# Second products of five groups by seven half-size products instead of eight blocks, with a new order of units around them

## The chip, the cores and the metric

The kernel runs on one core of a Trainium2 chip. The metric is the device time of one execution in microseconds; before the change it is 712.18 us (median of three runs, 710.34 to 712.77). The engines are written as the profile has them: PE multiplies matrices (PEld loads its weights), DVE and ACT do elementwise work and empty the PSUM banks, POOL and SP issue DMAs.

## The reference, cut to what matters

```python
mod = (silu(c) @ w_mod).reshape(c.shape[0], 6, 1, -1)
sa, ca, ga, sb, cb, gb = (mod[:, n] for n in range(6))
h = layernorm(x) * (1 + ca) + sa
x = x + ga * A(h)            # y = Re(DFT_seq(DFT_hidden(h))), as four matrix products
h = layernorm(x) * (1 + cb) + sb
x = x + gb * B(h)
# B: gate = h @ w1; up = h @ w3; out = (silu(gate) * up) @ w2
```

S = 2048 rows, D = 512, F = 1792, all float32. The change lies in B alone: in the product with w2, which this text calls the second product. The products with w1 and w3 are the first products.

## The kernel before

Every operand of a product is split into a high part (a rounding to the PE's format, written by ACT) and a low part (the rest, by a subtraction on DVE), and each product is three passes: high x high, high x low, low x high (line 100). In B the 1792 columns are seven groups g of 256, the rows four tiles t of 512, taken as two pairs: pair 0 is tiles 0 and 2, pair 1 is tiles 1 and 3. Twelve of the fourteen (g, pair) are **items**, which run last: item 0 to 4 are groups 2 to 6 of pair 0, item 5 to 11 are groups 0 to 6 of pair 1. Item 5 is called `turning` in the code.

The first products of an item use Strassen's scheme in Winograd's form: `factor` (line 1239 on) makes seven products for w1 (named a1 to a7 here, `kind` "a") and seven for w3 (b1 to b7), each of six 128x512 matmuls. Products 1, 6, 7, 4 add up in one PSUM bank (a **chain**), 5 and 3 in another, 2 in a third. Between two members of a chain the partial sum is taken out of the bank: after 1, 5 and 6 by an ACT copy to a tile `x`, after 2, 3 and 7 by a DVE addition, after 4 by the consumer itself. So the next member waits for the engine that empties the bank. `weight_jobs` prepares the weights of that scheme: `h` and `l` (the raw weight), and `sh` and `sl` (four sums of quarters, made by `totals` on DVE).

The second product of an item is eight blocks (`down_unit`): for each of two tiles and four output blocks d, two inner halves of three passes, six matmuls into one bank. ACT scales the bank by gb into half of a tile y (line 335); after every second block POOL issues a DMA that adds y (512 KB) to the running sum of the output in DRAM (`sums`, line 1146). Groups 5 and 6 of pair 1 (`own`) don't go through DRAM: DVE adds them to tiles `xr`, which SP reads back from `sums` once group 4 is through (`load_sums`), and which SP stores to the output at the end.

What is called a **unit** here is six 128x512 matmuls: a first product or a block y. The order of units is written out by hand, item by item, in the strings `head` and `body` near the end ("a6 a5 y a7 y y ...": a and b are first products, "-b7" is one of the item before, y the next second product in the queue `seconds`). Each unit issues its matmuls, then what empties its bank; `behind(n, f)` puts a piece of work n units later; `jobs` is a queue of weight preparation from which `beside` takes as DVE and ACT have credit. Tiles are slots of 4 KB per partition, 50 in all, given back and taken again in turn; whoever writes into a slot waits for the last reader of the tile before, which for a y is its DMA. `down_banks` names the banks of the second product (6 and 7 in this part).

Of the kernel before, what the change touches and what calls it, by code (L numbers as in the profile page):

```python
# [8 lines left out]
F32 = mybir.dt.float32  # L9
# [33 lines left out]
def folded(nc, pools, c, cp, wmr, wmc, x, xt, ctr, cti, wdr, wdi, w1, w3, w2, out):  # L43
# [51 lines left out]
    def times(dst, a, b):  # L95
        nc.vector.tensor_tensor(out=dst, in0=a, in1=b, op=OP.mult)  # L96
# [1013 lines left out]
        nc.sync.dma_start(to, sums[t, i])  # L1110

    ys = {}
    down_banks = [4, 4]

    def down_unit(g, pair, t, d, key):
        last = g == NG - 1

        own = pair == 1 and g >= NG - 2
        if not own and d % 2 == 0:
            ys[0] = take(F32, "y")  # L1120

        parts = 2 if own and last and (t, d) == (NT - 1, ND - 1) else 1
        for n in range(parts):
            at = slice(n * N // parts, (n + 1) * N // parts)
            to = bank(down_banks[0] + turn[1] % down_banks[1])[:, at]
            turn[1] += 1
            for q in range(2):
                product(
                    to,
                    [u[:, q, cols(d)] for u in wuse[key]],  # L1130
                    [hf[g, t, q][:, b, at] for b in range(2)],
                    q == 0,
                    q == 1,
                )
            if own:
                xs = xr[t][d // 2][:, d % 2, at]
                nc.vector.scalar_tensor_tensor(
                    xs, to, gb[:, d : d + 1], xs, op0=OP.mult, op1=OP.add
                )
# [68 lines left out]
    TO = {1: 0, 6: 0, 7: 0, 4: 0, 2: 1, 5: 2, 3: 2}  # L1208
    state, vs = {}, {}

    def right(pair, n):
        t0, t1 = PAIRS[pair]
        if n in (1, 2, 3):
            at = {1: (t0, 0), 2: (t0, 1), 3: (t1, 1)}[n]
            return h2h[at], h2l[at]
        at = pair, {5: 1, 6: 2, 7: 3, 4: 4}[n]
        return th[at], tl[at]

    def result(i, w, q, k, src):

        g, pair = items[i]
        v = vs[i][q][:, k, :]
        if w == "w1":
            behind(k != 0 or q == 0, lambda: nc.scalar.activation(v, src, AF.Silu))  # L1224
            return
        times(v, v, src)

        def highs():
# [8 lines left out]
        behind(2, lows)  # L1237

    def factor(i, w, n):
# [37 lines left out]
        if n == 3:  # L1277
            for x in wuse.pop(key).values():
                give(x)
            behind(1, lambda: give(st["x"]))  # L1280
            if w == "w3":
                for x in vs.pop(i):
                    behind(3, lambda x=x: give(x))


    loads.extend((n, m) for n in range(len(steps)) for m in range(2))
# [289 lines left out]
                up_block(g, t, q, w)  # L1576
                beside(2.72, USED[w])

    def down(g, pair, t, d, key):
        drain(lambda: (key, "l") in done, jobs)  # L1580
        delayed()
        down_unit(g, pair, t, d, key)
        beside(1.36, USED["own" if pair == 1 and g >= NG - 2 else "y"])

    for w in ("w1", "w3"):
# [17 lines left out]
        give(h.pop((2, 0)))  # L1603


    down_banks[:] = [6, 2]
# [4 lines left out]
    def other_operands():  # L1611
# [6 lines left out]
                give(h.pop((0, n)))  # L1618
        sum_parts(jobs, *sums_of.pop())

    def unit(kind, i, n):
        g, pair = items[i]
        more = i + 1 < len(items)
        if n == 1:
            drain(lambda: ("ready", i, "w1" if kind == "a" else "w3") in done, jobs)
        if (kind, i, n) == ("a", 0, 6):
            drain(lambda: ("t", 0, 4) in done)
        if (kind, i, n) == ("a", turning, 1):
            drain(lambda: not background)
        if kind == "a" and i == turning and n in (4, 5, 6, 7):  # L1630
            drain(lambda: ("t", 1, {6: 2, 5: 1, 7: 3, 4: 4}[n]) in done, jobs)
        delayed()
        factor(i, "w1" if kind == "a" else "w3", n)
        if (kind, n) == ("a", 1) and more:
            load_w(("w1", *items[i + 1]))
        if (kind, n) == ("a", 6):
            load_w(("w2", g, pair))
        if (kind, n) == ("a", 3) and more:
            load_w(("w3", *items[i + 1]))
            weight_jobs(i + 1, "w1")  # L1640
        if (kind, n) == ("b", 2):
            plain_jobs(("w2", g, pair))
        if (kind, n) == ("b", 3):
            if i + 2 == turning:
                drain(lambda: ("xc", 3) in done)
                for at in ((1, 0), (1, 1), (3, 1)):
                    chunk_parts(background, *at, 3)
                sums_of.append(pair_sums(background, 1))
            if i + 1 == turning:
                other_operands()  # L1650
            if more:
                weight_jobs(i + 1, "w3")
            for t in PAIRS[pair]:
                seconds.extend((g, pair, t, d, ("w2", g, pair)) for d in range(ND))
        beside(1.36, FACTOR[kind][n])

    weight_jobs(0, "w3")
# [822 lines left out]
```

## Time and profile before

| | us |
|---|---|
| three runs | 710.34, 712.77, 712.18 |
| median | 712.18 |
| profiled execution | 708.46 |
| its span, first to last instruction | 706.7 |
| mean granted PE clock over the span | 0.991 |
| PE busy in the span | 686.3 |
| DVE busy | 548.3 |
| ACT busy | 430.8 |

The profile comes from one execution with its own time, so changes are worked out against its span and then set against the median. A group line of the profile has the line and engine, output <- input by tile names, the partitions x elements, the count, then busy time and the mean of one in ns. A timeline line has the start, the duration and the instruction. The last instruction that computes starts at 698.8 us; what follows is the store of the output.

### The profile page before, as it was taken

The page shows a single profiled execution, that of the slowest core. Times are in us where ns is not written, and L with a number is a line of the kernel's source. Part 1 is how long each engine was busy: PE and PEld are TensorE (multiplying, and loading weights), DVE is VectorE, ACT ScalarE, POOL GpSimd, SP SyncE. Part 2 cuts the span into 40 slices and gives each one's busy share as a digit, 9 for nine tenths or more (in the row PEclk, how much of TensorE's full clock was granted, in tenths as well). Part 3 has the DMA queues.
Part 4 walks back from the last instruction along what each step waited for, and adds up shares of the span by engine and source line. Part 5 has one row for each costly group of instructions (what it writes and reads, how often), then busy time and mean ns, then how long its engine had stood idle before and what let it go on. Part 6 is the DMA issues. An engine that isn't in the chain of part 4 may idle for free.

```text
span 706.7 us, 8912 instructions
## 1 busy us (share of the span) xinstructions
PE 686.3 (97%) x3152; PEld 564.7 (80%) x3152; DVE 548.3 (78%) x877; ACT 430.8 (61%) x709; POOL 119.4 (17%) x141
## 2 busy tenths in 40 slices
PE   7999999999999999899999999999999999999995
PEld 4898888888888888687888788787788888888784
DVE  5999679997999978579987886896865556664763
ACT  4998865545454655745677676867665565656420
POOL 1320253542524000200100101011010100101000
PEclk9999999999999999999999999999999999999998
DMA  8730299796678521522868558376763847537403
GB/s 266 211 120 1 77 373 328 251 307 229 207 283 287 168 86 41 92 58 64 209 114 199 89 130 153 61 156 137 239 136 73 180 62 175 111 69 162 137 0 124
DMA packets 38100, 108.93 MB, mean 154 GB/s; under 512 B 4896, under 2 KB 5152, under 8 KB 38048
## 3 DMA queue, kind: packets, MB, share of 16 engines
q0 software_dynamic: 12352, 43.00, 29.3%
q1 hardware_dynamic: 25264, 63.98, 27.5%
q10 hardware_dynamic: 432, 1.31, 0.5%
q8 instruction: 26, 0.43, 0.3%
q14 instruction: 26, 0.21, 0.1%
HBM read 76.81 MB, written 33.55 MB: 156 GB/s over the span
## 4 chain that ended last, share of the span: by engine, by line
PE 81%; DVE 7%; ACT 6%; issue 2%; DMA 2%; SPq 1%; ACTq 0%; DVEq 0%
PE bank L100 52%; PE bank L750 25%; PE bank L559 2%; PE bank L598 1%; DMA wmr<-in_wmr 1%; ACT xc L894 1%; PE bank L576 1%; DVE xc L96 1%; SPq L231 1%; ACT hf L87 1%; ACT y L335 1%; DVE v L96 0%; DVE hl L90 0%; ACT hm L501 0%; DMA w<-in_wdi 0%
## 5 line engine op out<-in xcount | busy, mean ns | idle before, releaser
L100 PE MATMUL bank<-hf,w2h 128*128 128x512 f32 (+1 forms) x452 | 140.9, 391 | 0.3
L1146 POOL DMA_DIRECT2D sum<-y x48 | 41.0, 855 | 390.1 <-ACT y L335 373.0
L100 PEld LDWEIGHTS bank<-hf,w2h 128*128 128x128 f32 x452 | 84.3, 188 | 22.1 <-DVE hf L90 3.4
L100 PE MATMUL bank<-hf,w2l 128*128 128x512 f32 (+1 forms) x226 | 87.6, 388 | 0.0
L87 ACT ACTIVATE hf<-v 128x512 fp32r<-128x512 f32 x56 | 35.3, 630 | 67.3 <-DVE v L96 62.7
L335 ACT ACTIVATE y<-bank,gb 128x512 f32<-128x512 f32 x96 | 64.9, 682 | 18.6 <-PE bank L100 18.3
L93 DVE TENSOR_TENSOR v<-bank,x 128x512 f32<-128x512 f32 x36 | 24.7, 685 | 34.9 <-PE bank L100 34.8
L750 PE MATMUL bank<-bh,us 128*128 128x512 f32 x128 | 49.9, 390 | 0.0
L93 DVE TENSOR_TENSOR x<-bank,x 128x512 f32<-128x512 f32 x36 | 24.7, 687 | 32.4 <-PE bank L100 28.7
L750 PE MATMUL bank<-bh,ul 128*128 128x512 f32 x128 | 49.8, 389 | 0.0
L750 PE MATMUL bank<-d,us 128*128 128x512 f32 x128 | 49.8, 389 | 0.0
L750 PE MATMUL bank<-d,uh 128*128 128x512 f32 x128 | 49.8, 389 | 0.0
L750 PE MATMUL bank<-l,us 128*128 128x512 f32 x128 | 49.8, 389 | 0.0
L750 PE MATMUL bank<-l,uh 128*128 128x512 f32 x128 | 49.8, 389 | 0.0
L100 PEld LDWEIGHTS bank<-hf,w2l 128*128 128x128 f32 x226 | 42.4, 188 | 8.4
L90 DVE TENSOR_TENSOR hf<-v,hf 128x512 fp32r<-128x512 f32 x56 | 38.5, 687 | 12.2 <-ACT hf L87 12.1
L170 POOL DMA_INDIRECT re<-in_ctr,mirror x32 | 35.8, 1117 | 66.2 <-DVE ul L90 39.5
L1224 ACT ACTIVATE v<-v 128x512 f32<-128x512 f32 x36 | 22.8, 632 | 38.8 <-DVE v L93 38.8
L87 ACT ACTIVATE x<-bank 128x512 f32<-128x512 f32 x72 | 41.4, 586 | 7.2 <-PE bank L100 6.5
L170 POOL DMA_INDIRECT im<-in_cti,mirror x32 | 32.7, 1023 | 35.3 <-PE bank L750 10.0
L100 PE MATMUL bank<-h2h,w1h 128*128 128x512 f32 x80 | 31.8, 397 | 1.5 <-ACT h2h L87 1.5
L100 PE MATMUL bank<-h2l,w1h 128*128 128x512 f32 x80 | 31.9, 399 | 0.8 <-DVE h2l L90 0.8
(246 smaller groups left out, 1775.2 us busy)
## 6 DMA issues: line engine op xcount, KB each, us to landing
sum<-y POOLq DMA_DIRECT2D x48, 512.0 KB, 5.6
w<-in_w SPq DMA_DIRECT2D x42, 512.0 KB, 4.5
re<-in_ctr SPq DMA_DIRECT2D x32, 256.0 KB, 5.0
im<-in_cti SPq DMA_DIRECT2D x32, 256.0 KB, 5.0
wmc<-in_wmc SPq DMA_DIRECT2D x8, 512.0 KB, 6.3
xr<-in_xt SPq DMA_DIRECT2D x8, 512.0 KB, 7.6
sum<-xr SPq DMA_DIRECT2D x8, 512.0 KB, 6.2
x<-in_x SPq DMA_DIRECT2D x11, 256.0 KB, 4.8
```

What stands on the lines that cost most here:

```text
L87: nc.scalar.activation(dst, src, AF.Copy, scale=scale)
L90: nc.vector.tensor_tensor(out=dst, in0=a, in1=b, op=OP.subtract)
L93: nc.vector.tensor_tensor(out=dst, in0=a, in1=b, op=OP.add)
L96: nc.vector.tensor_tensor(out=dst, in0=a, in1=b, op=OP.mult)
L100: nc.tensor.matmul(acc, lhs[a], rhs[b], start=first and n == 0, stop=last and n == len(PASSES) - 1, skip_group_check=more,)
L170: nc.gpsimd.indirect_dma_start(dst, None, rows, bass.IndirectOffsetOnAxis(ap=at, axis=0))
L231: queue.dma_start(raw_w[dt][q * 64 : (q + 1) * 64, m, :], w[i][par::2, q])
L335: nc.scalar.activation(dst, src, AF.Identity, scale=by)
L559: nc.tensor.matmul(halves(hb[k])[:, m, :], sides((hh, hl)[a][k])[:, dt, m, :], wu[dt][:, b, m, :], start=False, stop=dt % 2 == 1 and n == ...
L750: nc.tensor.matmul(acc[what, e], lhs, rhs, start=begin and i == 0, stop=(end or (turn and what == "x")) and i == len(terms) - 1, skip_grou ...
L1146: nc.gpsimd.dma_start(sums[t, d // 2], y, accum_op=OP.add)
L1224: behind(k != 0 or q == 0, lambda: nc.scalar.activation(v, src, AF.Silu))
```

## The change

For the five items (g, 1) with g = 0 to 4 (`SEVEN`) the second product is made in the same Strassen form, over the two tiles, the two inner halves and the two halves of the output: seven products of two 128-column pieces, three passes each, so again six 128x512 matmuls in a unit, but seven units in place of eight. `ORDER7` is 2, 5, 3, 1, 6, 7, 4. Each unit fills two banks (6 and 7); 1, 6, 7, 4 add up in them and so do 5 and 3. After every unit ACT scales both banks into a whole y, and POOL adds that y to the sums in DRAM. The right operands need four differences and seven splits (`seven_parts`) where there were four splits, and w2 is prepared by five steps (`seven_jobs`) where there were two.

The order of units around it is rewritten: in most of these items two first products stand between two y, seven y are spread over the second part of one item and the start of the next, a3 stands ahead of a4, and the weights of w3 are prepared from b6 on rather than from b3 of the item before (`early_w3`). At the end w2 of the last group is loaded at a1 instead of a6, and once the last first product of w1 is through, the second product turns over five banks.

```diff
-    down_banks = [4, 4]
+    down_banks = [4, 5, 6, 7]
...
-            to = bank(down_banks[0] + turn[1] % down_banks[1])[:, at]
+            to = bank(down_banks[turn[1] % len(down_banks)])[:, at]
...
+    SEVEN = [(g, 1) for g in range(NG - 2)]
+    ORDER7 = (2, 5, 3, 1, 6, 7, 4)
+    LEFT7 = {1: "h0", 2: "h2", 4: "h3", 5: "s0", 6: "s1", 7: "s2", 3: "s3"}
+    TO7 = {2: (0, 0), 5: (1, 1), 3: (0, 1), 1: (0, 0), 6: (0, 1), 7: (1, 1), 4: (1, 0)}
...
+    def seven_parts(i, q, k):
...
+        if (q, k) != (0, 1):
+            n = {(0, 0): 1, (1, 0): 2, (1, 1): 3}[q, k]
+            behind(1, lambda: high(n, v[q, k]))
+            behind(2, lambda: low(n, v[q, k]))
+            return
+        t1, t2, t3, t4 = v[0, 0], v[1, 1], v[0, 1], v[1, 0]
+        behind(1, lambda: minus(t1, v[0, 1], v[0, 0]))
+        behind(2, lambda: high(5, t1))
+        behind(2, lambda: minus(t3, v[1, 1], v[0, 1]))
+        behind(3, lambda: low(5, t1))
+        behind(3, lambda: minus(t2, v[1, 1], t1))
+        behind(4, lambda: high(7, t3))
+        behind(4, lambda: minus(t4, v[1, 0], t2))
+        behind(5, lambda: high(6, t2))
+        behind(5, lambda: low(7, t3))
+        behind(6, lambda: high(4, t4))
+        behind(7, lambda: low(6, t2))
+        behind(8, lambda: low(4, t4))
...
+    def seven_jobs(key):
...
+        step(jobs, 1, highs, 0.0, 1.0)
+        step(jobs, 1, totals, 1.4)
+        step(jobs, 1, lows, 1.2)
+        step(jobs, 1, sum_highs, 0.0, 1.0)
+        step(jobs, 1, sum_lows, 1.2)
...
+    def seven_unit(g, pair, n, key):
+        new = n in (1, 2, 5)
+        if new:
+            banks7[:] = [bank(6), bank(7)]
+        y = take(F32, "y")
...
+        for e, to in enumerate(banks7):
+            at = int(LEFT7[n][1]) * HALF + e * P
+            product(
+                to,
+                [flat(wuse[key][x])[:, at : at + P] for x in names],
+                [u[:, b, :] for b in range(2)],
+                new,
+                True,
+                not new,
+            )
+            d = 2 * which + e
+            copy_by(y[:, e, :], to, gb[:, d : d + 1])
+        give(u)
+        nc.gpsimd.dma_start(sums[t, which], y, accum_op=OP.add)
+        behind(4, lambda: give(y))
+        if n == ORDER7[-1]:
...
+            if g == NG - 3:
+                for t in PAIRS[pair]:
+                    load_sums(t)
...
+    def early_w3(i):
+        return items[i][1] == 1
...
-        if (kind, n) == ("a", 1) and more:
-            load_w(("w1", *items[i + 1]))
+        if (kind, n) == ("a", 1):
+            load_w(("w1", *items[i + 1]) if more else ("w2", g, pair))
...
+        if not more and kind == "a" and state[i, "w1"]["n"] == 7:
+            down_banks[:] = [6, 7, 0, 1, 2]
-        if (kind, n) == ("a", 3) and more:
+        if (kind, n) == ("a", 7 if i == turning else 3) and more:
...
         body = "a6 a5 y a7 y y a4 y a3 y b1 y b2 y b6 b5 y"
+        if i and items[i - 1] in SEVEN:
+            body = "a6 a5 a7 y a3 a4 y b1 b2 y b6 b5 y"
+        spread = i > 1 and items[i - 2] in SEVEN
+        if spread and i < len(items) - 1:
+            body = body.replace("a6", "a6 y", 1)
+        if i == len(items) - 2:
+            body = "a6 y a5 y a7 a3 y a4 b1 y b2 b6 y b5"
...
         if i == len(items) - 1:
-            body = "a6 a5 y a7 y y a4 y a3 b1 y b2 b6 b5 y b7 y b4 y b3 y y y y y y y y"
+            body = "a6 a5 a7 a3 a4 b1 b2 y b6 y b5 y b7 y b4 y y b3 y y y y y y y y y y"
         head = "-b7 a1 -b4 -b3 a2 " if i == turning else "-b7 a1 a2 -b4 -b3 " if i else "a1 a2 "
+        if spread and i < len(items) - 1:
+            head = "-b7 a1 y a2 -b4 y -b3 "
+        if i == len(items) - 1:
+            head = "-b7 y a1 a2 y -b4 y -b3 "
```

Three places show what moves. The first is PE in item 7, where two blocks y of group 1 stand side by side before (banks 770 and 772; w2h and w2l are the parts of w2, hf the two inner halves):

```order
L100 MATMUL bank_770_4903<-hf_4764,w2h_4760 128x512 x2
L100 MATMUL bank_770_4903<-hf_4764,w2l_4762 128x512
L100 MATMUL bank_770_4903<-hf_4841,w2h_4760 128x512 x2
L100 MATMUL bank_770_4903<-hf_4841,w2l_4762 128x512
L100 MATMUL bank_772_4913<-hf_4764,w2h_4760 128x512 x2
```

The same item after the change, its product 5 and the first row of what follows:

```order
L100 MATMUL bank_789_4982<-hf_4900,w2sh_4773 128x512 x2
L100 MATMUL bank_789_4982<-hf_4900,w2sl_4783 128x512
L100 MATMUL bank_790_4983<-hf_4900,w2sh_4773 128x512 x2
L100 MATMUL bank_790_4983<-hf_4900,w2sl_4783 128x512
L100 MATMUL bank_793_4996<-h2h_4158,w3h_4785 128x512
```

A unit keeps its six matmuls, has one right operand in place of two, and fills two banks in place of one.

The second place is ACT in item 6, the first item with seven products, around the rounding of w2 (`w2h`). Before (y is the scaling of one bank, x the copy inside a first chain, hf a high part, w1sh the high part of the sums of w1):

```order
L335 ACTIVATE y_4718<-bank_735_4719,gb 128x512
L87 ACTIVATE w1sh_4729<-w1s_4712 128x1024
L87 ACTIVATE x_4738<-bank_738_4731 128x512
L335 ACTIVATE y_4718<-bank_741_4742,gb 128x512
L87 ACTIVATE w2h_4760<-w_719_4632 128x1024
L87 ACTIVATE hf_4764<-v_4583 128x512
L335 ACTIVATE y_4766<-bank_747_4767,gb 128x512
```

After, from product 5 (y_4721) to product 3 (y_4761):

```order
L335 ACTIVATE y_4721<-bank_739_4719,gb 128x512
L335 ACTIVATE y_4721<-bank_740_4720,gb 128x512
L87 ACTIVATE x_4741<-bank_743_4734 128x512
L87 ACTIVATE w2h_4752<-w_723_4644 128x1024
L87 ACTIVATE hf_4759<-v_4599 128x512
L335 ACTIVATE y_4761<-bank_739_4719,gb 128x512
L335 ACTIVATE y_4761<-bank_740_4720,gb 128x512
L87 ACTIVATE w2sh_4773<-w2s_4754 128x1024
```

Product 3 adds into bank 739, which product 5 filled, so its matmuls come after ACT's first row here; two scalings stand where one stood, and the rounding of w2's sums is new.

The third place is POOL's queue for group 1, the adding DMAs to the sums. Before:

```order
L1146 DMA sum_0_3300<-y_4886 128x1024
L1146 DMA sum_1_3302<-y_4912 128x1024
L1146 DMA sum_0_3799<-y_4954 128x1024
L1146 DMA sum_1_3801<-y_5002 128x1024
```

After:

```order
L1338 DMA sum_0_3300<-y_4940 128x1024
L1338 DMA sum_1_3801<-y_4984 128x1024
L1338 DMA sum_0_3799<-y_5023 128x1024
L1338 DMA sum_0_3300<-y_5065 128x1024
L1338 DMA sum_0_3799<-y_5105 128x1024
L1338 DMA sum_1_3801<-y_5133 128x1024
L1338 DMA sum_1_3302<-y_5165 128x1024
```

Four transfers become seven of the same size, and three of the four sums are added to twice.

More of the change, by code (lines that the diff above doesn't have):

```diff
@@ L1237, in result, with high, low @@
         behind(2, lows)
+    def seven_parts(i, q, k):
+        key = items[i]
+        v = {(a, b): vs[i][a][:, b, :] for a in range(2) for b in range(2)}
+        def high(n, src):
+            right7[key, n] = take(F32R, "hf")
+            copy(right7[key, n][:, 0, :], src)
+        def low(n, src):
+            u = right7[key, n]
+            minus(u[:, 1, :], src, u[:, 0, :].bitcast(F32))
+        if (q, k) != (0, 1):
+            n = {(0, 0): 1, (1, 0): 2, (1, 1): 3}[q, k]
+            behind(1, lambda: high(n, v[q, k]))
+            behind(2, lambda: low(n, v[q, k]))
+            return
+        t1, t2, t3, t4 = v[0, 0], v[1, 1], v[0, 1], v[1, 0]
[11 more added lines that the diff above has]
+        behind(8, lambda: low(4, t4))
@@ new lines, in seven_jobs, with highs, totals, lows @@
+    def seven_jobs(key):
+        use = wuse[key] = {}
+        def highs():
+            use["h"] = take(F32R, "w2h")
+            copy(flat(use["h"]), flat(wraw[key]))
+        def totals():
+            use["s"] = take(F32, "w2s")
+            s, r = four(use["s"]), four(wraw[key])
+            plus(s[:, 0, :], r[:, 1, :], r[:, 3, :])
+            minus(s[:, 1, :], s[:, 0, :], r[:, 0, :])
+            minus(s[:, 2, :], r[:, 0, :], r[:, 1, :])
+            minus(s[:, 3, :], r[:, 2, :], s[:, 1, :])
+        def lows():
+            use["l"] = take(F32R, "w2l")
+            r = wraw.pop(key)
+            minus(flat(use["l"]), flat(r), flat(use["h"]).bitcast(F32))
+            give(r)
+        def sum_highs():
+            use["sh"] = take(F32R, "w2sh")
+            copy(flat(use["sh"]), flat(use["s"]))
+        def sum_lows():
+            use["sl"] = take(F32R, "w2sl")
+            minus(flat(use["sl"]), flat(use["s"]), flat(use["sh"]).bitcast(F32))
+            give(use.pop("s"))
+            done.add((key, "l"))
+        step(jobs, 1, highs, 0.0, 1.0)
[3 more added lines that the diff above has]
+        step(jobs, 1, sum_lows, 1.2)
@@ new lines, in seven_unit @@
+    def seven_unit(g, pair, n, key):
[3 more added lines that the diff above has]
+        y = take(F32, "y")
+        which, k = TO7[n]
+        t = PAIRS[pair][k]
+        names = ("h", "l") if LEFT7[n][0] == "h" else ("sh", "sl")
+        u = right7.pop(((g, pair), n))
+        for e, to in enumerate(banks7):
[14 more added lines that the diff above has]
+        if n == ORDER7[-1]:
+            for x in wuse.pop(key).values():
+                give(x)
+            if g == NG - 3:
+                for t in PAIRS[pair]:
+                    load_sums(t)
@@ L1282, in factor @@
                 for x in vs.pop(i):
-                    behind(3, lambda x=x: give(x))
+                    behind(9 if items[i] in SEVEN else 3, lambda x=x: give(x))
     loads.extend((n, m) for n in range(len(steps)) for m in range(2))
@@ L1641, in unit @@
         if (kind, n) == ("b", 2):
-            plain_jobs(("w2", g, pair))
+            (seven_jobs if (g, pair) in SEVEN else plain_jobs)(("w2", g, pair))
         if (kind, n) == ("b", 3):
@@ L1650, in unit @@
                 other_operands()
-            if more:
+            if more and not early_w3(i):
                 weight_jobs(i + 1, "w3")
-            for t in PAIRS[pair]:
-                seconds.extend((g, pair, t, d, ("w2", g, pair)) for d in range(ND))
+            if (g, pair) in SEVEN:
+                seconds.extend((g, pair, n, ("w2", g, pair)) for n in ORDER7)
+            else:
+                for t in PAIRS[pair]:
+                    seconds.extend((g, pair, t, d, ("w2", g, pair)) for d in range(ND))
+        if (kind, n) == ("b", 6) and more and early_w3(i):
+            weight_jobs(i + 1, "w3")
         beside(1.36, FACTOR[kind][n])
```

17 lines of the change are left out of this document (13 added, 4 removed).

## The prediction

> **What bounds the kernel now.** I read the page first, then the waits of PE in the part that changes, then the stretches of single items, then the timeline.
>
> ```profile
> PE 686.3 (97%) x3152; PEld 564.7 (80%) x3152; DVE 548.3 (78%) x877; ACT 430.8 (61%) x709; POOL 119.4 (17%) x141
> ```
>
> PE is busy for 97% of 706.7 us. Over 471 to 700 us, where the change works, the waits of PE are one row:
>
> ```profile
> PE bank L100 <- DVE w1l L90: 0.2, 1, 0.2
> ```
>
> So PE sets the end there, and everything else hides. One item a row (columns: PE, PEld, DVE, ACT, POOL busy with counts, granted clock, DMA share, GB/s):
>
> ```profile
> 533.30:563.50 30.20, 30.20 (x134) 24.70 (x133) 17.85 (x27) 18.25 (x27) 3.44 (x5) 1.00 0.59 123
> 563.50:593.70 30.20, 30.20 (x134) 24.73 (x133) 17.85 (x27) 18.24 (x27) 3.44 (x5) 1.00 0.59 122
> 593.70:623.80 30.10, 30.10 (x133) 24.66 (x132) 17.85 (x27) 18.23 (x27) 3.34 (x5) 1.00 0.58 121
> ```
>
> An item takes 30.2 us at full clock, DVE and ACT work 60% of it, the DMA engines 59%.
>
> **What a unit is worth.** Two blocks y with one first product between them:
>
> ```profile
> 581.42 0.61 PE L100 MATMUL bank<-hf,w2h 128*128 128x512 f32 x2
> ...
> 582.78 0.39 PE L100 MATMUL bank<-h2h,w3h 128*128 128x512 f32 x1
> ...
> 584.14 0.61 PE L100 MATMUL bank<-hf,w2h 128*128 128x512 f32 x2
> ```
>
> 584.14 - 581.42 = 2.72 us for two units, so a unit costs 1.36 and a matmul 0.227 us, though each is shown 0.39 long: they overlap. The change removes one unit of eight in five items: 5 x 1.36 = 6.80 us.
> The Trainium skill (Perfetto Trace Analysis, Identifying the Most-Contended Engine) says that matmul busy time is a poor measure, since matmuls are pipelined. By the rows' durations the 30 matmuls would be worth 30 x 0.39 = 11.7 us; the starts agree with the rule, and 6.80 stands.
>
> **A stall that goes.** 22 units are 29.92 us, not 30.2. The rest is here, once an item:
>
> ```profile
> 571.65 0.62 PE L100 MATMUL bank<-hf,w2h 128*128 128x512 f32 x2
> 572.33 0.84 PE L100 MATMUL bank<-hf,w2h 128*128 128x512 f32 x2
> 573.25 0.39 PE L100 MATMUL bank<-th,w1sh 128*128 128x512 f32 x1
> PEld bank L100 <- DVE hf L90: 1.5, 4, 0.4
> ```
>
> The first y of an item takes 1.60 us, 0.24 over a unit: its second half waits for the low part that DVE makes right after b3 of the item before (last row: four items, four times). In the new order the first y of a group comes three or more units after b3 and reads product 2's operand, which is made of b4. Items 6 to 11 are six, 6 x 0.24 = 1.4 us; bounds 0 (a new lateness takes its place) and 1.4. I take 1.4 and count new stalls apart.
>
> **Five banks at the end** touch the last units only, where two banks run out:
>
> ```profile
> 697.11 0.40 PE L100 MATMUL bank<-hf,w2h 128*128 128x256 f32 x2
> 697.35 0.28 PE L100 MATMUL bank<-hf,w2l 128*128 128x256 f32 x1
> 697.77 0.50 PE L100 MATMUL bank<-hf,w2h 128*128 128x256 f32 x2
> 698.78 0.48 DVE L1137 SCALAR_TENSOR_TENSOR xr<-bank,gb,xr 128x256 f32<-128x256 f32 x1 [0.63 <-PE bank L100]
> ```
>
> The last half starts at 697.77 where 697.35 + 0.12 (half a pass) was due: 0.3 us. The 7.4 us from DVE's end (699.3) to 706.7 are the store and stay.
>
> **What is added.** By item of seven: ACT six more scalings, three more high parts, one rounding of sums; DVE four differences and three low parts more, the four sums of w2 and their low part; POOL three more transfers. The rows (533 to 654 us, and one group of sums):
>
> ```profile
> L335 ACT ACTIVATE y<-bank,gb 128x512 f32<-128x512 f32 x32 | 21.9, 684 | 8.3 <-PE bank L100 8.2
> L87 ACT ACTIVATE hf<-v 128x512 fp32r<-128x512 f32 x16 | 10.1, 634 | 18.6 <-DVE v L96 17.3 <-issue 1.3
> L87 ACT ACTIVATE x<-bank 128x512 f32<-128x512 f32 x24 | 14.1, 585 | 3.1 <-PE bank L100 3.1
> L1224 ACT ACTIVATE v<-v 128x512 f32<-128x512 f32 x12 | 7.6, 633 | 12.9 <-DVE v L93 12.9
> L87 ACT ACTIVATE w1sh<-w1s 128x1024 fp32r<-128x1024 f32 x4 | 4.3, 1063 | 0.5
> L90 DVE TENSOR_TENSOR hf<-v,hf 128x512 fp32r<-128x512 f32 x16 | 11.0, 686 | 2.8 <-ACT hf L87 2.8
> L90 DVE TENSOR_TENSOR w1sl<-w1s,w1sh 128x1024 fp32r<-128x1024 f32 x4 | 4.9, 1225 | 0.0
> 571.27 0.42 DVE L90 TENSOR_TENSOR w3s<-w 128x256 f32<-128x256 f32 x1
> ```
>
> ACT: 6 x 0.684 + 3 x 0.634 + 1.063 = 7.07, so 18.24 + 7.07 = 25.3 us. DVE: 7 x 0.686 + 4 x 0.42 + 1.225 = 7.71, so 25.6. Against 21 x 1.36 = 28.56 us for PE, both are at 89%: they still fit, and cost PE something only where they bunch. Two such places I worked through in order of issue.
>
> Product 3 adds into the banks of product 5, two units later. ACT works from product 2's y to product 5's first scaling through: silu, y, y, hf, w1h, hf, silu, silu, w1sh. With rows of 0.684 for y, 0.634 for hf and for silu, 1.06 for both w1: 6.65 us. In item 6 the silu can start only 2.4 us after a7, because DVE has the low parts of b3 and b4, two differences and w3's last low part to do before a7's addition; 2.4 + 6.65 + 0.68 = 9.7 us, and product 3 is due six units after a7, at 8.16: a stall of 1.55. Instructions of ACT start before the former has ended (next rows, 0.58 apart for 0.69), which saves some 0.1 each and leaves 0.9 to 1.0. I take 1.0, bounds 0 and 1.6.
>
> ```profile
> 610.43 0.69 ACT L335 ACTIVATE y<-bank,gb 128x512 f32<-128x512 f32 x1 [0.76 <-PE bank L100]
> 611.01 1.05 ACT L87 ACTIVATE w1h<-w 128x1024 fp32r<-128x1024 f32 x1
> ```
>
> In items 7 to 9 a7's addition is not late (1.0 after a7) and one hf fewer stands there: 1.0 + 6.0 + 0.68 = 7.7, under 8.16, no stall. The next tight place is b7, which adds to the bank that ACT copies after b6. Ahead of that copy ACT has an hf that waits for b2's multiplication (1.7 us after b2, since DVE first ends w1's last low part), then y, y and w2's rounding: 1.7 + 0.63 + 1.37 + 1.06 + 0.59 = 5.4 us after b2, and b7 is due four units after b2, at 5.44. One DVE instruction more ahead of it (0.69) makes it 0.7 late, overlapped starts make it 0.3 early: over five items 0 to 3.5. I take 0.2 each, 1.0, nearer to the overlapping rows. In the last item a7 stands one unit behind a6, whose copy waits behind an hf that waits for b3: 0.3. Outside these places the 7 us that each engine gains lie under PE's 28.56 us; what PE has to wait for in one such item counts about five times.
>
> **DMA.** One item before (547 to 577.2 us, queue q0 holds the adding transfers, q1 the loads):
>
> ```profile
> q0 software_dynamic: 576, 2.10, 44.7%
> q1 hardware_dynamic: 432, 1.57, 14.5%
> sum<-y POOLq DMA_DIRECT2D x4, 512.0 KB, 6.5
> w<-in_w SPq DMA_DIRECT2D x3, 512.0 KB, 5.9
> ...
> xr<-sum SPq DMA_DIRECT2D x4, 512.0 KB, 3.8
> ```
>
> 44.7% of 30.2 us / 4 = 3.38 us of all 16 engines for a transfer, 14.5% / 3 = 1.46 for a load. After: 7 x 3.38 + 3 x 1.46 = 28.0 of 28.56 us. That is thin cover. Between 455 and 500 us eight such transfers took less:
>
> ```profile
> q0 software_dynamic: 1149, 4.19, 54.6%
> ```
>
> 54.6% of 45 / 8 = 3.07, hence 25.9 us. A transfer is late for somebody only when its y's slot is wanted: product 6's y takes the slot of product 3's, six units (8.16 us) on, against some 1.2 us until issue and 6.5 to landing. I take zero, bounds 0 and the rival below. Reading the sums back (3.8 us a load, last row above, of 455 to 660 us) is issued eight units before the first xr is used, and that xr needs a sum that was finished earlier: zero, and rival three if not. SP's queue:
>
> ```profile
> 652.56 7.38 SPq L1106 DMA_DIRECT2D xr<-sum  x2
> 660.04 0.38 SPq L1035 DMA_DIRECT2D w<-in_w  x1
> ```
>
> The last load (w2 of group 6) stood behind two of these reads; at a1 it is ahead of all four, which wait for the seventh transfer. Left at a6 it would land some 14 us after product 4 (1.2 + 6.5 + 5.9), and b2 wants it eight units after, at 10.9; so the move averts a loss and gains nothing over before. w3 is loaded at a3 and first read six units on, after b6: 8.2 us against 5.9 to landing, hidden by 2 us.
>
> **Sum.** -6.80 - 1.4 - 0.3 + 1.0 + 1.0 + 0.3 = -6.2 us: span 700.5 for 706.7. The profiled execution, 708.46, lies 3.7 under the median, so I set the difference against the median: 712.18 - 6.2 = **706.0 us**. Own range: nothing stalls, 712.18 - 8.5 = 703.7; all stalls at their upper bounds (1.6 + 3.5 + 0.6) and the hf stall replaced, 712.18 - 1.4 = 710.8.
>
> **Rivals.**
> *ACT and DVE pace the items.* For: 89% each, in-order, each waiting for the other (the row of hf above: 17.3 us of ACT idle on DVE). Against: the two places worked out. It decides when ACT's scaling ends later than 2.72 us after its unit; if every item of seven so loses the unit it saved, 1.36 a time, only the 1.4 + 0.3 are left, less 1.0 for item 6: 711.5, no change.
> *The adding transfers become the bound (slower).* Late transfers hold y slots, ACT waits before a scaling, the banks stay full, PE stops. It decides above 28.56 us of DMA work an item and turns the sign when an item passes 30.2 us, that is 7a + 4.4 > 30.2, a = 3.69 us a transfer, 9% over 3.38. For: a lies at the edge and loads run beside. Against: the 3.07. With a = 3.9 an item is 31.7 us, five items +7.5, less 1.7: 718.
> The Trainium skill (Perfetto Trace Analysis, Identifying the Most-Contended Engine) calls DMA occupancy misleading with 16 engines and goes by HBM utilization; by that the new rate, 10 x 0.52 MB in 28.56 us or some 184 GB/s, would not bind. The page's row of slices has 373 GB/s as its fastest, which agrees; the chance below goes by the 3.07 alone.
>
> ```profile
> GB/s 266 211 120 1 77 373 328 251 307 229 207 283 287 168 86 41 92 58 64 209 114 199 89 130 153 61 156 137 239 136 73 180 62 175 111 69 162 137 0 124
> ```
>
> *The ends go wrong.* The seventh sum lands late, DVE waits for xr with PE's last chains behind it, some 3 to 5 us: 710. Against: the eight units above.
> That the change doesn't do what it says can be left out: the order of PE has the seven units.
>
> **Chances.** Forecast 0.64, ACT and DVE 0.16, DMA 0.13, the ends 0.07. This measurement tells 0.3%, 2.1 us, from no change: faster means under 710.0, slower over 714.3. Faster: 0.64 and about half of the ends and a third of ACT/DVE, 0.73. Same 0.13, slower 0.14 (DMA, and a little of the ends). The range takes the forecast and ACT/DVE: 703.5 to 713.
>
> **What would show it.** Right: 30 matmuls fewer; items 7 to 9 of about 28.6 us with PE without a gap; DVE and ACT near 25 us in them; DMA share 0.9 to 0.98; a single gap of about 1 us in item 6 ahead of product 3 with ACT y as releaser. Wrong: PE waits for ACT y or x in every item (first rival), ACT idle on a DMA ahead of a scaling and landings beyond 9 us (second), DVE idle ahead of the first xr (third).

## The result, and the profile after

The changed kernel takes **704.63 us** (703.37 to 705.38) where the kernel before took 711.89 (710.34 to 712.77) on the same chip: a ratio of 0.9909, with a 95% interval of 0.9891 to 0.9927. That is 5.2 to 7.8 us. The forecast was 706.0.

The page of the changed kernel, its row of engines:

```profile
PE 678.3 (97%) x3122; PEld 557.8 (80%) x3122; DVE 583.0 (83%) x937; ACT 456.5 (65%) x759; POOL 135.1 (19%) x156
```

PE has 30 matmuls fewer, DVE 60 instructions and ACT 50 more. PE is as full as before: it still sets the end. Three stretches of an item's length from item 7 on (PE, PEld, DVE, ACT, POOL busy with counts, granted clock, DMA share, GB/s):

```profile
534.40:563.00 28.60, 28.60 (x128) 23.66 (x127) 24.96 (x40) 23.63 (x38) 5.98 (x7) 1.00 0.94 186
563.00:591.50 28.50, 28.50 (x127) 23.64 (x126) 24.74 (x40) 23.34 (x38) 5.97 (x7) 1.00 0.92 181
591.50:620.10 28.60, 28.60 (x127) 23.68 (x127) 24.84 (x40) 23.45 (x38) 5.98 (x7) 1.00 0.94 189
```

PE has no gap in them, DVE and ACT stand at 87% and 82% of the item. The waits of PE from 471 us to the end:

```profile
PE bank L100 <- ACT y L335: 0.6, 1, 0.6
PE bank L100 <- ACT x L87: 0.3, 1, 0.3
```

There are two, and both were named beforehand. The first is product 3 in item 6, the second a7 in the last item:

```profile
522.26 0.73 PE L100 MATMUL bank<-hf,w2sh 128*128 128x512 f32 x2 [0.55 <-ACT y L335]
...
657.32 0.50 PE L100 MATMUL bank<-th,w1sh 128*128 128x512 f32 x1 [0.28 <-ACT x L87]
```

**A finer measure than the span.** Up to item 5 all the kernels here run the same order on PE, yet item 5's a1 starts anywhere from 469.89 to 474.10 us in their profiled executions. That is as much as most of the effects. So the kernels are compared below by the time from item 5's a1 to PE's last matmul, in the one profiled execution of each. For the changed kernel these are the rows:

```profile
473.11 0.39 PE L100 MATMUL bank<-h2h,w1h 128*128 128x512 f32 x1
...
692.76 0.28 PE L100 MATMUL bank<-hf,w2l 128*128 128x256 f32 x1
```

692.76 - 473.11 = 219.65 us. Before it is 698.47 - 471.88 = 226.59. The change is worth 6.94 us there. Item 5, whose order on PE is the same in all the kernels, takes 30.73 to 31.01 us from its a1 to item 6's, so a difference of some 0.3 us by this measure tells nothing by itself. The profiled spans differ by 5.1 only (706.7 and 701.6), since that execution came to item 5 1.2 us later and its last store ended 0.6 us later after PE.

All kernels by this measure, with the ratio of the whole time to the kernel before where it was timed several times (rest_w3_at_b3 and two_banks were timed once and are read by their traces alone):

| kernel | us from item 5's a1 to the last matmul | items 8 and 9, us each | ratio to before (95%) |
|---|---|---|---|
| before | 226.59 | 30.2 | 1 |
| changed | 219.65 | 28.6 | 0.9909 (0.9891 to 0.9927) |
| rest_only | 223.90 | 29.9 | 0.9959 (0.9943 to 0.9975) |
| rest_w3_at_b3 | 225.71 | 30.2 | |
| w3_at_b3 | 229.13 | 30.4 | 1.0034 (1.0016 to 1.0051) |
| old_order_w3 | 229.38 | 31.1 | 1.0039 (1.0022 to 1.0056) |
| w2_late | 220.32 | 28.6 | 0.9907 (0.9879 to 0.9934) |
| two_banks | 220.07 | 28.6 | |
| dma_plus3 | 220.43 | 28.6 | 0.9933 (0.9900 to 0.9967) |
| dma_plus7 | 238.02 | 32.4 | 1.0158 (1.0119 to 1.0197) |
| act_plus7 | 229.28 | 30.1 | 1.0040 (1.0026 to 1.0054) |
| moved | 219.85 | 28.6 | 0.9910 (0.9894 to 0.9926) |
| last_moved | 218.52 | 28.6 | 0.9905 (0.9887 to 0.9924) |
| last_w1 | 217.63 | 28.6 | 0.9888 (0.9868 to 0.9908) |

### The profile page after: what moved, and what is told of

Its sections match the earlier page's. It is cut to its first block, busy times and chain, and to the rows that moved or that the text cites. A ratio compares the mean times of both kernels' runs of the same rounds, so it can differ in the third digit from the quotient of the medians.

```text
span 701.6 us, 9014 instructions
## 1 busy us (share of the span) xinstructions
PE 678.3 (97%) x3122; PEld 557.8 (80%) x3122; DVE 583.0 (83%) x937; ACT 456.5 (65%) x759; POOL 135.1 (19%) x156
## 4 chain that ended last, share of the span: by engine, by line
PE 79%; DVE 9%; ACT 7%; issue 3%; DMA 1%; another core or an unknown queue 1%; SPq 0%; ACTq 0%; DVEq 0%
PE bank L100 50%; PE bank L750 25%; PE bank L559 2%; PE bank L598 1%; ACT xc L894 1%; DVE v L96 1%; ACT y L335 1%; ACT hf L87 1%; DMA x<-in_x 1%; DVE xc L96 1%; DVE x L93 1%; DVE st L449 1%; PE bank L485 1%; DVE ul L90 1%
## 5 line engine op out<-in xcount | busy, mean ns | idle before, releaser
L100 PE MATMUL bank<-hf,w2h 128*128 128x512 f32 (+1 forms) x352 | 108.5, 389 | 0.1
L335 ACT ACTIVATE y<-bank,gb 128x512 f32<-128x512 f32 x126 | 81.6, 682 | 8.1 <-PE bank L100 7.8
L87 ACT ACTIVATE hf<-v 128x512 fp32r<-128x512 f32 x71 | 44.3, 630 | 62.8 <-DVE v L96 57.5
L100 PEld LDWEIGHTS bank<-hf,w2h 128*128 128x128 f32 x352 | 65.6, 188 | 15.8 <-ACT y L335 1.4
L1146 POOL DMA_DIRECT2D sum<-y x28 | 24.1, 859 | 247.6 <-ACT y L335 234.4
L100 PE MATMUL bank<-hf,w2l 128*128 128x512 f32 (+1 forms) x176 | 68.1, 387 | 0.0
L90 DVE TENSOR_TENSOR hf<-v,hf 128x512 fp32r<-128x512 f32 x71 | 48.9, 688 | 14.3 <-ACT hf L87 14.3
L1338 POOL DMA_DIRECT2D sum<-y x35 | 29.9, 854 | 128.8 <-ACT y L335 124.3
L100 PEld LDWEIGHTS bank<-hf,w2l 128*128 128x128 f32 x176 | 33.0, 188 | 6.7
L93 DVE TENSOR_TENSOR v<-bank,x 128x512 f32<-128x512 f32 x36 | 24.8, 688 | 16.3 <-PE bank L100 15.4
```

The lines of the kernel that those rows point to most:

```text
L87: nc.scalar.activation(dst, src, AF.Copy, scale=scale)
L90: nc.vector.tensor_tensor(out=dst, in0=a, in1=b, op=OP.subtract)
L93: nc.vector.tensor_tensor(out=dst, in0=a, in1=b, op=OP.add)
L100: nc.tensor.matmul(acc, lhs[a], rhs[b], start=first and n == 0, stop=last and n == len(PASSES) - 1, skip_group_check=more,)
L335: nc.scalar.activation(dst, src, AF.Identity, scale=by)
L1338: nc.gpsimd.dma_start(sums[t, which], y, accum_op=OP.add)
```

## The experiments

### The units alone, and what stood beside them: rest_only, rest_w3_at_b3

```diff
-    SEVEN = [(g, 1) for g in range(NG - 2)]
+    SEVEN = []
...
-        if i and items[i - 1] in SEVEN:
-            body = "a6 a5 a7 y a3 a4 y b1 b2 y b6 b5 y"
...
+        if i > turning:
+            body = "a6 a5 y a7 y y a3 y a4 y b1 y b2 y b6 b5 y"
```

The heads and the last item's order went back as well. a3 stays ahead of a4, and w1 for item 6 is still prepared from a7 of item 5 on rather than from a3.

> No item uses seven products: all keep eight blocks y, in the order of before (a3 ahead of a4 after the turning item); the early preparation of w3, the early last load of w2 and the five banks at the end stay. Theory (PE sets the end and the removed units carry the gain): five units come back, 6.8 us, and the hf stall of 0.24 us an item with them; items 7 to 9 last 30.2 us again, the time is 711 to 712, the only thing won over before the 0.3 us of the last bank stall. Rival (the earlier preparation and loads carry a good part of the gain): 706 to 709, with items under 30.0 us.

It is 0.41% faster than before, where next to nothing was expected: 223.90 us for 226.59. The items have lost the hf stall though every y is back in its old place. PE in item 8, the first y of the item:

```profile
570.07 0.62 PE L100 MATMUL bank<-hf,w2h 128*128 128x512 f32 x2
...
571.43 0.39 PE L100 MATMUL bank<-th,w1sh 128*128 128x512 f32 x1
```

571.43 - 570.07 = 1.36 us, a plain unit, where it took 1.60. What was left of the change had to be doing it, and the early preparation of w3 was the first candidate. So that alone was undone as well:

```diff
     def early_w3(i):
-        return items[i][1] == 1
+        return False
```

> No item uses seven products (as in the run with eight blocks everywhere), and w3 is prepared from b3 on as well. Theory one (w3's jobs ahead of the low parts make the hf stall): the stall is back, items 7 to 9 last 30.2 us. Rival (another part, such as a3 ahead of a4, removed it): 29.9 us.

The stall is back, and so are the items of 30.2 us:

```profile
563.30:593.50 30.20, 30.20 (x134) 24.73 (x133) 17.86 (x27) 18.24 (x27) 3.44 (x5) 1.00 0.58 121
```

DVE shows why. In rest_w3_at_b3, in the same item:

```profile
569.65 0.69 DVE L96 TENSOR_TENSOR v<-v,x 128x512 f32<-128x512 f32 x1
570.26 0.42 DVE L93 TENSOR_TENSOR w3s<-w 128x256 f32<-128x256 f32 x1
...
571.39 0.42 DVE L90 TENSOR_TENSOR w3s<-w,w3s 128x256 f32<-128x256 f32 x1
571.73 0.69 DVE L90 TENSOR_TENSOR hf<-v,hf 128x512 fp32r<-128x512 f32 x1
```

and in rest_only:

```profile
568.27 0.69 DVE L96 TENSOR_TENSOR v<-v,x 128x512 f32<-128x512 f32 x1
568.88 0.68 DVE L90 TENSOR_TENSOR hf<-v,hf 128x512 fp32r<-128x512 f32 x1
```

Between b3's multiplication and the low part that the first y wants stand the four sums of w3: the low part starts 2.08 us after the multiplication in the one and 0.61 in the other. The two kernels differ by 225.71 - 223.90 = 1.81 us, which is the price of w3's place in an eight-block kernel. The remaining 0.88 from before to rest_w3_at_b3 is a wait for w1's low part at item 6's start (0.55 us of lost PE time by the starts of its matmuls) and the last bank stall. DVE makes that low part at 502.17 us in the kernel before and at 494.41 in rest_w3_at_b3, where w1 is prepared from a7 on; no run undoes that edit alone.

### The order of the units: old_order_w3

```diff
-            body = "a6 a5 a7 y a3 a4 y b1 b2 y b6 b5 y"
...
+            body = "a6 a5 y a7 y y a4 y a3 y b1 y b2 y b6 b5"
```

The heads with a y in them and the last item's order went too.

> Seven products everywhere the change has them, but PE's units stand in the order of before, with the eighth y left out of the items after turning; heads and the last item's body are those of before too. So products 5 and 3 follow each other without the two units between them. Theory (a following product must wait for ACT's scaling of the bank it adds to): PE waits for ACT y in each item of items 7 to 9, 1 to 2 us per item, and the saving of 6.8 us shrinks to between 0 and 3: 708 to 714. Rival (the spacing does not matter, ACT has 3 to 4 us of idle time in an item): 704.6, items of 28.6 us.

It is slower than before, with 30 matmuls fewer. Items last 31.1 us, 2.5 more than in the changed kernel. The waits of PE from 471 us on:

```profile
PE bank L100 <- ACT y L335: 5.7, 5, 1.6
PE bank L100 <- ACT x L87: 3.2, 4, 0.8
```

Two products in a row, in item 8:

```profile
575.20 0.61 PE L100 MATMUL bank<-hf,w2sh 128*128 128x512 f32 x2
...
576.32 1.25 ACT L335 ACTIVATE y<-bank,gb 128x512 f32<-128x512 f32 x2
577.04 0.73 PE L100 MATMUL bank<-hf,w2sh 128*128 128x512 f32 x2 [1.00 <-ACT y L335]
```

Product 5 ends at about 575.9, ACT begins its scaling at 576.32 behind a silu, and product 3 can only add to bank 6 once that is read, at 577.04. The two units between products are what hides this in the changed kernel. By the starts of the matmuls this place costs about half of the 2.5 us; the rest of it is b7, which waits 0.81 us in the same item for ACT's copy of b6 (the second row of waits). The rival, that ACT's idle time is enough in any order, has fallen.

### w3 prepared from b3 on, with seven products: w3_at_b3

The edit is that of `early_w3` above, alone.

> The changed kernel with one part undone: w3's operands of the next item are again prepared from b3 on, not after b6. The eight-block run without seven products lost the hf stall although its first y still came right behind b3, so theory one (DVE works at w3's sums ahead of the hf's low parts, and the earlier preparation of w3 is what removed the stall) says that bunches come back at the start of an item: with the first y three units after b3 there is no hf stall of 0.24 us, but the additions of a7 and product 5's operands are later, 0.3 to 1 us per item in items 7 to 9, ratio to before 0.993 to 0.997. Rival (the order of the units alone removed it, as the prediction has it): items 28.6 us as in the changed kernel, ratio 0.991.

It costs 9.48 us of 219.65, five times what the same edit costs with eight blocks, and the kernel is slower than before. PE's waits:

```profile
PE bank L100 <- DVE v L93: 4.2, 5, 1.8
PE bank L100 <- ACT y L335: 1.9, 3, 1.1
```

DVE in item 7 (of w3_at_b3), from w3's low parts to the addition of a7:

```profile
544.56 1.22 DVE L90 TENSOR_TENSOR w3l<-w,w3h 128x1024 fp32r<-128x1024 f32 x1
545.70 0.69 DVE L90 TENSOR_TENSOR v<-v,v 128x512 f32<-128x512 f32 x1
546.30 1.22 DVE L90 TENSOR_TENSOR w3sl<-w3s,w3sh 128x1024 fp32r<-128x1024 f32 x1
...
549.37 0.68 DVE L93 TENSOR_TENSOR v<-bank,x 128x512 f32<-128x512 f32 x1
```

In the changed kernel the same addition waits for PE, not PE for it:

```profile
543.54 0.69 DVE L93 TENSOR_TENSOR v<-bank,x 128x512 f32<-128x512 f32 x1 [0.65 <-PE bank L100]
```

PE in the same item, the first y of the group (product 2) and the wait of a4, which adds to the bank of a7:

```profile
546.40 0.67 PE L100 MATMUL bank<-hf,w2h 128*128 128x512 f32 x2
...
547.84 0.39 PE L100 MATMUL bank<-h2h,w1sh 128*128 128x512 f32 x1
...
550.11 0.50 PE L100 MATMUL bank<-th,w1h 128*128 128x512 f32 x1 [0.72 <-DVE v L93]
```

Product 2 takes 1.44 us here, 0.08 over a unit, so at that y the new order alone removes nearly all of the hf stall of 0.24 us, as the expectation said. The lateness of DVE comes out behind it.

The differences of the seven products and the sums of w3 both fall due after b3. In this order of its queue DVE does not get both done in time. The stall that the range of the expectation named (0.3 to 1 us an item) was 1.8: 30.4 for 28.6. About 1.0 of it stands ahead of a4, the rest at a later product and at b7, behind ACT.

### The last w2, and the banks: w2_late, two_banks

```diff
-        if (kind, n) == ("a", 1):
-            load_w(("w1", *items[i + 1]) if more else ("w2", g, pair))
+        if (kind, n) == ("a", 1) and more:
+            load_w(("w1", *items[i + 1]))
```

> The last w2 (group 6, pair 1) is loaded at a6, as before, and not at a1. Theory: in the queue of SP it stands behind reads of sums that wait for the seventh adding transfer, lands some 14 us after product 4 while its y units want it 10.9 us after: PE waits about 3 us in the last item, 707.5. Rival (the reads are over sooner, the load hides): 704.6.

The load does land late, and ACT and DVE do wait for it (640 to 700 us):

```profile
ACT w2h L87 <- DMA w<-in_w: 5.1, 1, 5.1
DVE w2l L90 <- ACT w2h L87: 3.9, 1, 3.9
```

ACT gets it at 666.64, some 16 us after product 4 has ended; 14 were worked out. But PE loses 0.5 us in the last item (47.99 for 47.49), not 3, most of it in one wait:

```profile
PE bank L100 <- DVE x L93: 0.4, 1, 0.4
```

The first y with that w2 stands some ten units further on in the order of PE, near 680 us; the y up to there use group 5's w2. The 10.9 us were the time at which the preparation is queued, not the time at which PE needs it, and what stands behind it on ACT and DVE was nearly all covered. By the whole time it cannot be told from the changed kernel.

```diff
-            down_banks[:] = [6, 7, 0, 1, 2]
+            down_banks[:] = [6, 7]
```

> The last units keep two banks instead of five. Theory: PE waits 0.3 us for DVE's reading of a bank ahead of the last half block, as before, and the end is 0.3 us later, seen in the trace alone. Rival (with every y of the last item now in a row at the end, two banks run out at each block): several waits for DVE or ACT, 1 us or more together.

The old gap is back, and it is the only one at the end:

```profile
688.85 0.28 PE L100 MATMUL bank<-hf,w2l 128*128 128x256 f32 x1
689.26 0.50 PE L100 MATMUL bank<-hf,w2h 128*128 128x256 f32 x2
```

688.85 + 0.12 was due, 689.26 it became: 0.29 us, as forecast.

### What DMA can take: dma_plus3, dma_plus7

```diff
         nc.gpsimd.dma_start(sums[t, which], y, accum_op=OP.add)
+        if n in (5, 1, 7):
+            nc.gpsimd.dma_start(spare[g, n], y)
```

In dma_plus7 each product does it.

> The changed kernel with three more writes per item of seven: y of products 5, 1 and 7 goes also as a plain 512 KB write to DRAM that nobody reads. Occupancy view: 26.5 us of DMA work in an item of 28.56 become 26.5 + 3 x 1.4 = 30.7, the items are DMA-bound, +2.1 us x 5, ratio to before about 1.005. Bandwidth view (the Trainium skill, Perfetto Trace Analysis, Identifying the Most-Contended Engine): some 240 GB/s, still far under the 373 seen elsewhere, nothing happens, 0.991.

> The same with a spare write of each y, seven per item. Occupancy view: 26.5 + 7 x 1.4 = 36.3 us of DMA work in an item, +7.7 us x 5, ratio about 1.045. Bandwidth view: some 310 GB/s, no change, 0.991.

Neither view has it. Three more transfers an item (dma_plus3, items 7 to 9):

```profile
530.40:559.40 29.00, 28.88 (x127) 23.58 (x126) 24.98 (x41) 23.55 (x38) 7.60 (x10) 1.00 1.01 238
559.40:588.00 28.60, 28.60 (x128) 23.68 (x127) 24.84 (x41) 23.42 (x38) 7.63 (x10) 1.00 1.03 240
588.00:616.50 28.50, 28.50 (x127) 23.63 (x126) 24.74 (x40) 23.21 (x38) 7.61 (x10) 1.00 1.01 239
```

The share is over 1, and in items 8 and 9 PE has no gap: 240 GB/s fit there. So the 3.07 to 3.38 us of packet time that the prediction books for a transfer are not what it costs; 92 to 94% of the changed kernel's items was not an edge. It is near one, though: item 7 is 0.4 us longer than in the changed kernel, lost at one product whose bank ACT empties late, and ACT waited there for the landing of an adding transfer:

```profile
535.39 1.27 ACT L335 ACTIVATE y<-bank,gb 128x512 f32<-128x512 f32 x2 [0.36 <-DMA sum<-y]
```

Seven more (dma_plus7) do not fit:

```profile
560.30:591.60 31.30, 28.83 (x127) 23.57 (x126) 24.76 (x40) 23.14 (x38) 9.90 (x14) 1.00 1.03 278
591.60:625.00 33.40, 30.49 (x127) 24.71 (x127) 24.78 (x40) 23.33 (x38) 9.90 (x14) 0.95 1.05 276
```

ACT's waits in items 7 to 9, and the spare writes of items 7 and 8 with their median time to landing:

```profile
ACT y L335 <- DMA spare<-y: 8.6, 3, 3.4
```

```profile
spare<-y POOLq DMA_DIRECT2D x14, 512.0 KB, 9.9
```

ACT waits for the landing of a spare write before it may scale into that y's slot again, PE for ACT: the second rival's mechanism, at 276 GB/s and not at 184. In the second row the granted clock is 0.95, so part of that item's length, PE's 30.49 busy us for 28.83, is slower matmuls; the first row is at full clock. Items 7 to 9 last 32.4 us in the mean for 17 transfers of 0.52 MB (seven added, seven written, three loaded), so a transfer costs 1.9 us at most. At that price the changed kernel's ten take 19 of its 28.56 us. Whether the rate itself or the number of y slots sets the 276 was not told apart: the spare writes land 9.9 us after issue, longer than the 8.16 us after which their slot is wanted.

The Trainium skill (Perfetto Trace Analysis, Identifying the Most-Contended Engine) has it that the occupancy of 16 DMA engines misleads and that HBM utilization is to be used in its place; with a share of 1.03 and PE without a gap at 240 GB/s this case agrees with the first half. In dma_plus7 transfers did bind, well under the 373 GB/s that a slice of the page before reaches, so the fastest slice is no measure of what such a mix can hold.

### How much ACT has to spare: act_plus7

```diff
             copy_by(y[:, e, :], to, gb[:, d : d + 1])
+        copy_by(y[:, 1, :], banks7[1], gb[:, 2 * which + 1 : 2 * which + 2])
```

The scaling is repeated to the same place, so the values stay.

> The changed kernel with one ACT instruction more in each product of a seven-unit: bank 7's scaling is done twice, 7 x 0.69 = 4.8 us more of ACT in an item of 28.56 us of which 23.4 are busy: 28.2, 99%. Theory (ACT has cover on the average but not where it bunches; each following product waits for the scaling two units before it, and ACT needs 0.7 us more there): PE waits for ACT y or x in each item, 1 to 3 us per item, ratio 0.998 to 1.012. Rival (what is under 100% hides): 0.991.

Items last 30.1 us for 28.6, and the whole is 0.4% slower than before. ACT is busy for 28.6 of 31.0 us, a stretch a little longer than item 8:

```profile
562.00:593.00 31.00, 30.46 (x131) 24.08 (x130) 25.80 (x43) 28.64 (x47) 5.98 (x7) 1.00 0.91 174
```

4.8 us were added where 5.2 were idle, and 1.6 us came through to PE: the cover does not reach to the last tenth. PE's largest wait in items 7 to 9 is again ahead of b7, for ACT's copy of b6.

### The two gaps that are left: moved, last_moved, last_w1

```diff
+        if i == turning + 1:
+            body = "a6 a5 a7 y a3 a4 y b1 b2 b6 y b5 y"
...
-            body = "a6 a5 a7 a3 a4 b1 b2 y b6 y b5 y b7 y b4 y y b3 y y y y y y y y y y"
+            body = "a5 b1 a7 a3 a4 b2 y b6 y b5 y b7 y b4 y y b3 y y y y y y y y y y"
...
-            head = "-b7 y a1 a2 y -b4 y -b3 "
+            head = "-b7 y a1 a2 -b4 y -b3 a6 y "
```

> The changed kernel with the order changed in two places where PE still waits: in item 6 one unit more stands between products 5 and 3 (b6 goes ahead of the second y), in the last item a6 goes behind the y of product 4 and a5, b1 ahead of a7, so that each bank is scaled before it is added to. Theory (PE sets the end, so a stall taken away is time gained): the 0.55 us ahead of product 3 and the 0.3 ahead of a7 are gone, some of the small ones of the last item too: 0.8 to 1.2 us off, ratio to before 0.989 to 0.990. Rival (the lateness moves to the next unit that depends on ACT, as its queue is no shorter): as the changed kernel, 0.991.

The sum is that of the changed kernel, because one edit won what the other lost. The last item went from 47.49 to 46.19 us. Item 6 went from 25.78 to 27.05:

```profile
523.51 0.50 PE L100 MATMUL bank<-th,w3sh 128*128 128x512 f32 x1 [1.61 <-ACT x L87]
```

b6 adds to a bank that ACT copies after product 5's scaling, so it now takes the wait, and a longer one. For item 6 the rival was right. last_moved keeps the two edits of the last item (its body and its head) and leaves item 6 as in the changed kernel:

> The changed kernel with the last item's order alone changed (a6 behind the y of product 4, a5 and b1 ahead of a7); item 6 is as in the changed kernel. In the run that moved both places the last item took 46.19 us from its a1 to PE's last matmul for 47.49, and item 6 27.05 for 25.78, so the two cancelled. Theory (the items add up, as PE is the only thing that passes time on): 1.3 us off the changed kernel, 218.35 us from item 5's a1 to the last matmul for 219.65, ratio to before 0.988 to 0.990. Rival (the last item started later in that run and its tail owes its speed to that): 219.65.

218.52 us: the theory, to 0.2 us. In last_w1 item 7's w1 is prepared later in addition:

```diff
             load_w(("w3", *items[i + 1]))
-            weight_jobs(i + 1, "w1")
+        if (kind, n) == (("b", 1) if i == turning + 1 else ("a", 7 if i == turning else 3)) and more:
+            weight_jobs(i + 1, "w1")
```

> The same, and in item 6 the preparation of w1 for item 7 is queued after b1 and not after a3. Two ACT instructions of 1.05 us (w1h, w1sh) stand ahead of product 5's scalings no more. Theory (product 3's wait of 0.55 us in item 6 is ACT's queue): the wait is gone, items 6 takes 25.2 instead of 25.8 us, 217.7 us in all, ratio 0.987 to 0.989. Rival (the work only moves, and w2's, w3's and w1's preparations bunch ahead of item 7): some 0.5 to 1.5 us of new waits at b6, b7 or item 7's a1, 218.5 to 219.5.

Item 6 has no gap left, and the last item has none. Both rows of last_w1:

```profile
505.10:529.60 24.50, 24.50 (x110) 20.27 (x109) 21.87 (x38) 17.45 (x30) 2.56 (x3) 1.00 0.62 156
...
645.50:691.70 46.20, 46.20 (x210) 38.44 (x210) 27.56 (x40) 14.70 (x24) 2.56 (x3) 1.00 0.49 125
```

It is 217.63 us for 219.65 (0.3 us of waits came up in item 7). Its ratio, 0.9888, beats the changed kernel's 0.9909, but the intervals overlap: that it is faster than the changed kernel rests on the trace, and that it beats the kernel before on both.

## Why the prediction was right, and where it was not

By the runs, undone in this order, the 6.94 us come about so: -6.80 for the units, -1.81 for w3's place, -0.88 for item 6's start and the last banks, and +2.55 for new waits (rest_only to changed: -4.25, where five units are -6.80, so the last figure is what is left; item 6 and the last item lose 1.3 us each by their lengths against last_w1, which has no gap in them).

- **-6.80 for five units:** right. Items 7 to 9 last 28.6 us, which is 21 x 1.36, and PE has 30 matmuls fewer. By the durations shown (0.39 a matmul) it would have been 11.7.
- **-1.4 for the hf stall:** right in size (1.81 with the last item's second one), and half of the account. The prediction put its end down to the new order, "the first y of a group comes three or more units after b3". The order does that at this y (w3_at_b3, 0.08 us over a unit for 0.24), but DVE's lateness then costs 1.8 us an item in other places. What made the stall is the four sums of w3 ahead of the low parts: rest_only keeps the old order and has no stall, rest_w3_at_b3 has it. The row that was quoted (PEld waits for DVE hf) named DVE, and the question that was not asked is what DVE was doing.
- **w3 at zero, "hidden by 2 us":** the step that failed. Only the load was priced, and it is indeed hidden. That the move also clears DVE right after b3 was left out. It is worth 1.81 us by itself and 9.48 in the changed kernel, which without it is slower than the kernel before. That the total came out all the same is luck: the 1.4 us that w3's place wins were in the sum under another name, and the loss that it averts was not looked for.
- **-0.3 for five banks:** right (0.29).
- **Item 6's start:** the prediction quotes PE's wait for w1's low part and gives it no term. It was worth 0.55 us, and it is gone with w1 prepared earlier in item 5 (argued from the times of the low part, not from a run of its own).
- **+1.0 in item 6 ahead of product 3:** right in place, cause and releaser; 0.55 us of wait (0.8 by the starts of the matmuls) within the bounds 0 to 1.6. ACT's queue stood there as it was worked out, but took 5.63 us from that silu (515.90) to product 5's scaling (521.53) where 6.65 were added up. last_w1 shows that it was ACT's queue: with w1's two high parts out of it the wait is gone.
- **+1.0 for b7 in five items:** nothing in items 7 to 9, 0.4 us in item 6 alone. The lower bound, overlapping starts, was the true one.
- **+0.3 for a7 in the last item:** right, 0.28. But the last item has 1.3 us of waits in all: products 7 and 4 also stand too close to the products before them. That was not worked through. It makes up for b7, so 2.55 us of new waits stand against 2.3 forecast: that the two agree is luck.
- **The first rival** (ACT and DVE pace the items) did not happen. DVE came out at 24.8 us an item for the 25.6 forecast, ACT at 23.4 for 25.3: the rows' durations were added up, and ACT's instructions overlap. But the rival was near in a way that its "89%" doesn't tell: undoing the order or w3's place, or 4.8 us more of ACT, brings it about, and each makes the kernel slower than before.
- **The second rival** (DMA) was judged by the wrong number. Its threshold of 3.69 us a transfer was in packet time, which dma_plus3 shows can go past the span of an item without harm to it, so the threshold says nothing.
- **The third rival** (a late read of the sums): DVE did not wait for it. The early load of w2 was forecast to avert a loss, and averts 0.5 us.

## What to carry to other kernels

When a wait is found, name what the releasing engine did just before: the remedy may be to move that work, and it may be in the change already under another name. Where a product adds into a bank that another engine must read first, what counts is the distance in units between the two, since the mean load of the reading engine (82% here) says nothing of it. Weigh a change of 1% from a fixed event that all versions share, item by item: the part ahead of it varied by 4.2 us here, with an effect of 7.

## What the hardware showed that was not expected

The DMA share of a stretch can exceed 1.0 without holding up PE: 1.01 to 1.03 at 240 GB/s in items 8 and 9 of dma_plus3 with PE full, against 0.92 to 0.94 at 181 to 189 GB/s in the changed kernel. The same share, 1.03, stands in item 8 of dma_plus7, at 278 GB/s and 2.8 us longer, so the share does not tell the two apart. One item of dma_plus3 lost 0.4 us at 238 GB/s, and every item from 7 to 9 stretched at 276 GB/s.
